# Recurrent attention and a feed-forward block on one core: the first four chunks' feed-forward by weight quarters, a listed order for the prologue, and products of zeros in TensorE's first waits

## The chip, the cores and the metric

The kernel runs on one core of a Trainium2 chip. A core has a matrix engine (TensorE, PE in the profile), VectorE (DVE), ScalarE (ACT), GpSimd (POOL) and a queue engine (SyncE, SP) that issues most of the DMAs here. The metric is the device time in microseconds (us), as the median of several runs. One more run was recorded by the hardware profiler, and all rows quoted here come from such records.

## The reference

The first part is a linear recurrence with a decay, for 4 sequences of 768 steps, 8 heads of 48. The second is a feed-forward block over all 3072 tokens, with `d_model` 384 and `d_ff` 2048.

```python
for t in range(S):
    cur = np.einsum('bhd,bhe->bhde', u[None] * kt, vt)
    y[:, :, t] = np.einsum('bhd,bhde->bhe', rt, state + cur)
    state = wt[:, :, :, None] * state + np.einsum('bhd,bhe->bhde', kt, vt)
x = y.transpose(0, 2, 1, 3).reshape(B * S, H * D)
h = x @ w_in
out = np.maximum(0.01 * h, h) @ w_out
```

Inputs and output are float32 in memory. The kernel's matrix products take bfloat16.

## The kernel before

**Chunks.** Each sequence is cut into chunks of 128 steps, 24 chunks in all. Within a chunk the recurrence becomes matrix products. The steps for one chunk are:

- load w, k, r and v (`load_in`, L470), 192 KB each;
- `lw`, the logarithm of w, on ACT (L332), and its running sum by a product with a triangle matrix, into the one bank `cp`;
- exponentials of the sum, `er` and `ek` (`grow`, L342, ACT), and the products `rk` = r x `er` and k x `ek` (`product`, L348, DVE);
- four transposes each of `rk` on PE (`turn`, L391) and their copies to `rkT` (DVE and ACT); from chunk 12 on a DMA transposes instead;
- scores (L750, or L629 in a pair), masked on DVE (`masked`, L412);
- the state, carried from chunk to chunk: an outer product on PE (L761, L594), `sb` = the decayed state (`shrink`, L421, POOL) and their sum (`state`, L434, DVE);
- the output product (L780 and L785; L646 and L654 in a pair) into the one bank `yp`, and the bonus of u: `ru` twice, `dg` and `vs` (`bonus`, L357 to L369, POOL and DVE), added in `finish` (L444, DVE);
- the transposed result `xT` (L458 on PE, L465 on ACT).

Chunks 0 and 1, and chunks 2 and 3, run as pairs, whose loads take rows of two steps (384 KB a load).

**Feed-forward.** For a chunk there are four *up* quarters and four *down* quarters. An up quarter (L821) is 12 matmuls 128x128, `w_in` against `xT`, into one of the two `hp` banks; ACT applies the leaky ReLU into `g` (L855). A down quarter (L873) is 4 matmuls of 384 columns, `g` against `w_out`, into one of the two `op` banks; after four of them the sum is copied to `o` and stored (L893).

**Weights.** `weight_steps` loads `w_in` and `w_out` in four quarters of 768 KB each, in float32, into buffers of the same ring as the inputs. Each quarter is cast in two halves, one on DVE (L313) and one on ACT (L315). The first down quarter needs the first quarter of `w_out`, the fourth needs the last.

**What sets the order.** Every step is entered in a `Plan` with its engine, an estimated duration, its dependencies and a priority. `Plan.order` runs through the steps in estimated time. On each engine the ready step with the lowest priority number starts next, and the instructions are then emitted in that order. On the chip each engine runs its instructions in the order that they were emitted and waits where an operand isn't there. Attention steps have priorities near ten times the chunk's number, feed-forward steps 1000 and more in an order `seq`: chunk n's ups alternate with chunk n-1's downs. `LEAD` keeps attention at most 8 chunks ahead. `WEIGHTS` tells at which chunk a weight quarter's steps are entered, and with which priority; here one `w_in` quarter comes between the second pair's loads (20.15), the other seven after them (24.0).

```python
PAIRS = (0, 2)
PWIRE, WIRE = 1.45, 1.15
WEIGHTS = [(2, 20.15)] + [(4, 24.0)] * 7
CASTS = 3
```

Of the kernel before, what the change touches and what calls it, by code (L numbers as in the profile page):

```python
# [15 lines left out]
class Plan:  # L16
# [5 lines left out]
    def __init__(self):  # L22
        self.eng, self.dur, self.fn, self.deps, self.pri, self.wire, self.rows = [], [], [], [], [], [], []

    def add(self, eng, dur, fn, deps, pri, wire=None, rows=0):

        i = len(self.eng)
        self.eng.append(eng)
        self.dur.append(dur)
        self.fn.append(fn)  # L30
        self.deps.append(sorted({d for d in deps if d is not None}))
        self.pri.append(pri)
        self.wire.append(wire)
        self.rows.append(rows)
        return i

    def order(self):
# [19 lines left out]
        while events:  # L57
# [13 lines left out]
            free[e] = now + self.dur[i] * (1.8 if e == "PE" and now < 26 else 1)  # L71
            if self.wire[i] is None:
                done[i] = free[e] + self.LAT[e]
            else:

                flying = [x for x in flying if x[0] > free[e]]
                while sum(x[1] for x in flying) + self.rows[i] > 3300:
                    free[e] = max(free[e], flying.pop(0)[0])
                dma_free = max(dma_free, free[e]) + self.wire[i]
                done[i] = dma_free + 1.6  # L80
                flying.append((done[i], self.rows[i]))
# [42 lines left out]
def kernel(  # L124
# [11 lines left out]
    nc = tc.nc  # L136
# [12 lines left out]
    NCI = 3  # L149
# [5 lines left out]
    PWIRE, WIRE = 1.45, 1.15  # L155
    WEIGHTS = [(2, 20.15)] + [(4, 24.0)] * 7
    CASTS = 3
    blocks = [1] * NCH
    assert sum(blocks) == NCH
# [9 lines left out]
    trex = pool.tile([128, 128], BF16, name="trex")  # L169
# [3 lines left out]
    pex = pool.tile([128, 128], BF16, name="pex")  # L173
    halves = pool.tile([128, 2], BF16, name="halves")
# [12 lines left out]
    er_r = ring("er", 3, [128, H, D], F32)  # L187
# [13 lines left out]
    g_r = ring("g", 3, [128, NJ, max(blocks) * L], BF16)  # L201
# [5 lines left out]
    yp_r = pp_r = ring("yp", 1, [128, 512], F32, psum)  # L207
# [3 lines left out]
    with tc.manual_schedule():  # L211
        nc.scalar.preload_act_table_set("natural_log_exp_and_others")

        for t, op in ((trev, ALU.is_ge), (trex, ALU.is_gt)):
# [26 lines left out]
        for q in (0, 64):  # L241
            for i, op in ((slice(0, 64), ALU.is_gt), (slice(64, 128), ALU.is_gt),
# [5 lines left out]
                )  # L248
        nc.vector.memset(onef[:], 1.0)
# [13 lines left out]
        def step(eng, dur, fn, pri, reads=(), writes=(), deps=(), wire=None, rows=0):  # L263
# [4 lines left out]
            i = plan.add(eng, dur, fn, d, pri, wire, rows)  # L268
            for x in (*reads, *writes):
                x.steps.append(i)  # L270
            return i

# [12 lines left out]
        def weight_steps(q, which, pri):  # L285
# [14 lines left out]
            ld = step("SP", 0.45, load, pri, writes=[st], wire=2.0, rows=(384, 512)[which])  # L300
            made = []
            for half, eng in ((0, "DVE"), (1, "ACT")):
                def cast(st=st, q=q, half=half, eng=eng):
# [8 lines left out]
                    if eng == "DVE":  # L312
                        nc.vector.tensor_copy(out=o, in_=i)  # L313
                    else:
                        nc.scalar.copy(out=o, in_=i)  # L315
                d = 0.8 if eng == "DVE" else 0.84
                made.append(step(eng, d, cast, CASTS, reads=[st], deps=[ld]))
# [17 lines left out]
        def cast_v(vb, vn, vl, P0):  # L335
            return step(
                "POOL", 0.57, lambda: nc.gpsimd.tensor_copy(out=vb.t[:], in_=vn.t),  # L337
                P0 + 2, reads=[vn], writes=[vb], deps=[vl])
# [6 lines left out]
        def product(rk, a, xn, e, P0, deps, n):  # L345
            return step(
                "DVE", 0.65 if n < 2 else 0.84 - 0.04 * a,
                lambda: nc.vector.tensor_tensor(out=rk.t[:, a, :, 0:D], in0=xn.t, in1=e.t[:], op=ALU.mult),  # L348
                P0, reads=[xn, e], writes=[rk], deps=deps)

        def bonus(vs, rn, kn, vn, loads, P0):
# [5 lines left out]
                lambda: nc.gpsimd.tensor_tensor(out=ru.t[:], in0=rn.t, in1=ubv, op=ALU.mult),  # L357
                P0 + 2, reads=[rn], writes=[ru], deps=[rl, u_ld])
            s_ruk = step(
                "POOL", 1.05,  # L360
                lambda: nc.gpsimd.tensor_tensor(out=ru.t[:], in0=ru.t[:], in1=kn.t, op=ALU.mult),  # L361
                P0 + 2, reads=[kn, ru], deps=[kl, s_ru])
# [6 lines left out]
                lambda: nc.gpsimd.tensor_tensor(  # L369
                    out=vs.t[:], in0=vn.t, in1=dg.t[:].unsqueeze(2).to_broadcast([128, H, D]), op=ALU.mult),  # L370
                P0 + 2, reads=[vn, dg], writes=[vs], deps=[vl, s_dg])
# [4 lines left out]
        def turn(rk, rkT, s_d, n, P0, banks):  # L376
# [8 lines left out]
            for a, eng in ((0, "DVE"), (1, "ACT")):  # L385
# [10 lines left out]
                def evac(trv=trv, a=a, eng=eng):  # L396
                    o, i = rkT.t[:, a * NP : (a + 1) * NP, :], trv[:, 0:NP, :]
                    if eng == "DVE":
                        nc.vector.tensor_copy(out=o, in_=i)
                    else:  # L400
                        nc.scalar.copy(out=o, in_=i)
# [3 lines left out]
                    eng, 0.42 if eng == "DVE" else 0.585, evac, P0, reads=[tr], writes=[rkT], deps=[s_tr]))  # L405
# [12 lines left out]
        def shrink(sb, s_in, a_ap, use, P0, deps):  # L418
            return step(
                "POOL", 0.92,  # L420
                lambda: nc.gpsimd.tensor_tensor(  # L421
                    out=sb.t[:].rearrange("p g a d -> p (g a) d"),
                    in0=s_in.t[:].rearrange("p g a d -> p (g a) d"),
                    in1=a_ap.rearrange("p g a -> p (g a)").unsqueeze(2).to_broadcast([128, H, D]),
                    op=ALU.mult),
                P0 + 1, reads=[s_in, use], writes=[sb], deps=deps)

        def state(sx, pp, i, sb, P0, deps):

            def f():  # L430
                if sb is None:
                    nc.vector.tensor_copy(out=sx.t[:], in_=i)
# [4 lines left out]
                "DVE", 0.55, f, P0 + 1, reads=[pp] + ([] if sb is None else [sb]), writes=[sx], deps=deps)  # L437

        def finish(yp, vs, s_y, s_vs, n, P0):
# [16 lines left out]
            def typose():  # L456
# [8 lines left out]
                lambda: nc.scalar.copy(out=xT[:, :, col : col + L], in_=trv[:, 0:KT, :]),  # L465
                P0 + 1, reads=[yp], deps=[s_yt]))
# [6 lines left out]
        def spread_u():  # L473
# [4 lines left out]
            up = op_r.take()  # L478
# [12 lines left out]
        def pair(n):  # L491
# [46 lines left out]
            er = [er_r.take() for _ in range(2)]  # L538
            ek = [ek_r.take() for _ in range(2)]
            if n < NCI:  # L540
                cs = [(hp_r if n == 0 else op_r).take() for _ in range(2)]
                s_c = [
                    step("PE", 0.33, lambda: sums(cs[0].t, pev, pev), P0, reads=lw, writes=[cs[0]], deps=s_ln),
                    step("PE", 0.33, lambda: sums(cs[1].t, pex, pex), P0, reads=lw, writes=[cs[1]], deps=s_ln)]
                e_in = [hd(x.t[:, 0:DM]) for x in cs]
                s_w = []
            else:
                cs = [ci_r.take() for _ in range(2)]
                s_c = [
                    step(  # L550
                        "DVE", dve(DM, 120),
                        lambda j=j: nc.vector.tensor_tensor(
                            out=cs[j].t[:], in0=hd(cp.t[:, 0:DM]), in1=lw[j].t[:, :, 0:D],
                            op=(ALU.subtract, ALU.add)[j]),
                        P0, reads=[cp, lw[j]], writes=[cs[j]], deps=[s_cum])
                    for j in range(2)]
                e_in = [x.t[:] for x in cs]
                s_w = s_c
            mid = hd(cp.t[:, 0:DM])
            s_er1 = grow(er[1], cp, mid, 1.0, P0, [s_cum, *s_w])  # L560
            s_ek0 = grow(ek[0], cp, mid, -1.0, P0, [s_cum, *s_w])
            s_er0 = grow(er[0], cs[0], e_in[0], 1.0, P0, [s_c[0]])
            s_ek1 = grow(ek[1], cs[1], e_in[1], -1.0, P0, [s_c[1]])
# [13 lines left out]
            for j in range(2):  # L577
                s_k = product(rk[j], 1, kn[j], ek[j], P0, [kl, (s_ek0, s_ek1)[j]], n)
                s_r = product(rk[j], 0, rn[j], er[j], P0, [rl, (s_er0, s_er1)[j]], n)
# [7 lines left out]
            pps = [op_r.take(), op_r.take()] if n == 0 else [se_r.take(), so_r.take()]  # L587
# [80 lines left out]
        def single(n):  # L668
# [34 lines left out]
            er, ek = er_r.take(), ek_r.take()  # L703
            if n < NCI:
                cq = op_r.take()
                s_ci = step(
                    "PE", 0.17,
                    lambda: nc.tensor.matmul(
                        hd(cq.t[:, 0:DM]), lhsT=trex[:], rhs=lw.t[:, :, 0:D], start=True, stop=True),
                    P0, reads=[lw], writes=[cq], deps=[s_ln])  # L710
                ci, e_in, s_w = cq, hd(cq.t[:, 0:DM]), [s_cum]
            else:
                ci = ci_r.take()
                s_ci = step(
                    "DVE", dve(DM, 120),
                    lambda: nc.vector.tensor_tensor(  # L716
                        out=ci.t[:], in0=hd(cp.t[:, 0:DM]), in1=lw.t[:, :, 0:D], op=ALU.add),
                    P0, reads=[cp, lw], writes=[ci], deps=[s_cum, s_ln])
                e_in, s_w = ci.t[:], [s_cum, s_ci]
            s_er = grow(er, cp, hd(cp.t[:, 0:DM]), 1.0, P0, s_w)  # L720
            s_ek = grow(ek, ci, e_in, -1.0, P0, [s_ci])
            rk = rk_r.take()
            s_r = product(rk, 0, rn, er, P0, [rl, s_er], n)
# [208 lines left out]
```

## Time and profile before

| what | us |
|---|---|
| median of 5 runs | 189.44 |
| lowest and highest of them | 188.65, 192.76 |
| the profiled execution | 188.68 |
| its span, first to last instruction | 187.0 |
| PE busy in the span | 175.0 |
| DVE, ACT, POOL busy | 130.9, 116.2, 109.1 |
| first load issued | 0.80 |
| first up quarter starts | 20.66 |
| first down quarter starts | 27.44 |
| first up quarter of chunk 4 starts | 50.13 |

A page of the profile gives the busy time of each engine, the span in 40 slices with the busy tenths of each engine, the chain of waits that ended last, and the costliest groups of instructions. A group's row names the line, the engine, the operation, what is written and read, how many there are, their busy time and the mean of one. The engine timelines give start and length of single instructions; a bracket at the end of a line is the idle time before it and what ended it. `SPq` is SyncE issuing a DMA. A matmul's end is modelled, so where matmuls follow each other their starts tell more than their lengths.

### The profile page before, as it was taken

To read this page: it belongs to the slowest core of one execution; us is meant where nothing else is said; L and a number is where in the kernel's file an instruction comes from. 1 tells how busy PE (TensorE), PEld (TensorE's weight loads), DVE (VectorE), ACT (ScalarE), POOL (GpSimd) and SP (SyncE) were. 2 spreads that over 40 slices of the span, in tenths; PEclk is the share of its full clock that TensorE was granted. 3 is DMA by queue.
4 is the path that set the end of the run, shared out by engine and by line. 5 is a ranking of instruction groups with operands and counts; after the bars stand their busy time and mean duration, and the time that the engine had idled before them with its cause. 6 is when DMAs were issued, how large, how long until landed. Compare 5 with 4: busy or idle time off the path is not lost.

```text
span 187.0 us, 6219 instructions
## 1 busy us (share of the span) xinstructions
PE 175.0 (94%) x2550; PEld 137.3 (73%) x2550; DVE 130.9 (70%) x226; ACT 116.2 (62%) x254; POOL 109.1 (58%) x148
## 2 busy tenths in 40 slices
PE   3678879999999999999999999999999999999992
PEld 1256767788778878788787787878887877877871
DVE  2399796777779888877967999766987868441111
ACT  2746686678876877796687666676374645334430
POOL 7799923277969798978792885172637644500000
PEclk9999999999999999999999999999999999999999
DMA  6999999999988897987899779998789995512102
GB/s 154 261 316 325 369 381 300 195 190 222 189 194 176 178 227 155 217 195 174 173 210 188 147 164 230 143 177 190 139 189 174 172 206 124 123 44 67 38 7 84
DMA packets 116383, 34.62 MB, mean 185 GB/s; under 512 B 109697, under 2 KB 114818, under 8 KB 116354
## 3 DMA queue, kind: packets, MB, share of 16 engines
q1 hardware_dynamic: 116352, 34.22, 84.2%
q8 instruction: 20, 0.33, 0.7%
q14 instruction: 9, 0.07, 0.1%
q10 hardware_dynamic: 2, 0.00, 0.0%
HBM read 25.17 MB, written 4.72 MB: 160 GB/s over the span
## 4 chain that ended last, share of the span: by engine, by line
PE 84%; SPq 7%; DMA 6%; DVE 1%; issue 0%
PE op L873 34%; PE hp L821 33%; DMA in<-in_moe_w_out_dram 6%; SPq L470 4%; PE se L750 3%; SPq L290 3%; PE yp L785 2%; PE cp L691 2%; PE yp L761 2%; PE yp L780 2%; PE se L391 1%; PE so L391 1%; PE yp L458 1%; PE cp L696 1%; DVE w_out_b L313 1%; PE yp L654 1%
## 5 line engine op out<-in xcount | busy, mean ns | idle before, releaser
L855 ACT ACTIVATE g<-hp 128x512 bf16<-128x512 f32 x96 | 57.0, 596 | 43.5 <-PE hp L821 42.5
L821 PE MATMUL hp<-xT,w_in_b 128*128 128x128 bf16 x1152 | 79.7, 220 | 0.1
L873 PE MATMUL op<-w_out_b,g 128*128 128x384 bf16 x384 | 76.5, 326 | 1.0 <-DVE w_out_b L313 1.0
L821 PEld LDWEIGHTS <-w_in_b 128*128 128x128 bf16 x1152 | 69.9, 98 | 7.1 <-DVE w_in_b L313 0.2
L873 PEld LDWEIGHTS <-g 128*128 128x128 bf16 x384 | 33.0, 97 | 15.8 <-issue 1.1
L357 POOL TENSOR_TENSOR ru<-in,ub 128x384 f32<-128x384 f32 x24 | 26.7, 1111 | 14.2 <-DMA in<-in_r_dram 14.1
L369 POOL TENSOR_TENSOR vs<-in,dg 128x384 f32<-128x384 f32 x24 | 20.2, 843 | 17.6 <-DVE dg L365 13.9
L361 POOL TENSOR_TENSOR ru<-ru,in 128x384 f32<-128x384 f32 x24 | 25.8, 1077 | 0.9
L421 POOL TENSOR_TENSOR sb<-s,a 128x384 bf16<-128x384 f32 x17 | 15.7, 926 | 16.4 <-DVE s L434 12.9
L348 DVE TENSOR_TENSOR rk<-in,er 128x384 bf16<-128x384 f32 x24 | 19.3, 803 | 7.5 <-DMA in<-in_r_dram 5.6
L348 DVE TENSOR_TENSOR rk<-in,ek 128x384 bf16<-128x384 f32 x24 | 23.3, 970 | 1.4 <-ACT a L738 0.9
L412 DVE TENSOR_TENSOR m<-se,maskb 128x512 bf16<-128x512 f32 x20 | 13.7, 687 | 7.5 <-PE so L750 6.9
L444 DVE TENSOR_TENSOR y<-yp,vs 128x384 bf16<-128x384 f32 x24 | 13.3, 552 | 7.7 <-PE yp L785 4.8
L889 DVE COPY o<-op 128x384 f32<-128x384 f32 x10 | 5.6, 556 | 17.1 <-PE op L873 17.0
L337 POOL CAST vb<-in 128x384 bf16<-128x384 f32 x24 | 15.4, 646 | 0.9 <-DMA in<-in_v_dram 0.9
L332 ACT ACTIVATE lw<-in 128x384 bf16<-128x384 f32 x24 | 12.4, 520 | 2.8 <-DMA in<-in_w_dram 2.6
L365 DVE TENSOR_REDUCE dg<-ru 128x8 f32<-128x384 f32 x24 | 12.9, 542 | 1.1 <-POOL ru L361 1.1
L412 DVE TENSOR_TENSOR m<-so,maskb 128x512 bf16<-128x512 f32 x20 | 13.6, 679 | 0.0
L342 ACT ACTIVATE er<-cp 128x384 f32<-128x384 f32 x22 | 10.8, 492 | 3.5 <-DVE ci L716 3.0
L716 DVE TENSOR_TENSOR ci<-cp,lw 128x384 f32<-128x384 f32 x20 | 11.0, 549 | 1.5 <-ACT g L855 0.9
L342 ACT ACTIVATE ek<-ci 128x384 f32<-128x384 f32 x20 | 10.5, 524 | 0.0
L391 PEld LDWEIGHTS <-rk 128*128 128x128 bf16 x96 | 6.9, 105 | 4.8 <-DVE rk L348 4.0
(103 smaller groups left out, 193.2 us busy)
## 6 DMA issues: line engine op xcount, KB each, us to landing
out_dram<-o SPq DMA_DIRECT2D x24, 192.0 KB, 2.2
in<-in_w_dram SPq DMA_DIRECT2D x20, 192.0 KB, 3.6
in<-in_k_dram SPq DMA_DIRECT2D x20, 192.0 KB, 3.8
in<-in_r_dram SPq DMA_DIRECT2D x20, 192.0 KB, 3.7
in<-in_v_dram SPq DMA_DIRECT2D x20, 192.0 KB, 3.5
in<-in_moe_w_in_dram SPq DMA_DIRECT2D x4, 768.0 KB, 8.5
in<-in_moe_w_out_dram SPq DMA_DIRECT2D x4, 768.0 KB, 12.4
in<-in_w_dram SPq DMA_DIRECT2D x2, 384.0 KB, 5.1
```

The lines of the kernel that those rows point to most:

```text
L337: "POOL", 0.57, lambda: nc.gpsimd.tensor_copy(out=vb.t[:], in_=vn.t),
L342: "ACT", 0.5, lambda: nc.scalar.activation(out=out.t[:], in_=i, func=AF.Exp, scale=scale),
L348: lambda: nc.vector.tensor_tensor(out=rk.t[:, a, :, 0:D], in0=xn.t, in1=e.t[:], op=ALU.mult),
L357: lambda: nc.gpsimd.tensor_tensor(out=ru.t[:], in0=rn.t, in1=ubv, op=ALU.mult),
L361: lambda: nc.gpsimd.tensor_tensor(out=ru.t[:], in0=ru.t[:], in1=kn.t, op=ALU.mult),
L369: lambda: nc.gpsimd.tensor_tensor(out=vs.t[:], in0=vn.t, in1=dg.t[:].unsqueeze(2).to_broadcast([128, H, D]), op=ALU.mult),
L412: lambda par=par: nc.vector.tensor_tensor(out=m.t[:, par], in0=gt(sc[par].t), in1=mask.unsqueeze(1).to_broadcast([128, NP, 128]), op=ALU.m ...
L421: lambda: nc.gpsimd.tensor_tensor(out=sb.t[:].rearrange("p g a d -> p (g a) d"), in0=s_in.t[:].rearrange("p g a d -> p (g a) d"), in1=a_ap ...
L444: lambda: nc.vector.tensor_tensor(out=y.t[:], in0=hd(yp.t[:, 0:DM]), in1=vs.t[:], op=ALU.add),
L821: nc.tensor.matmul(hp.t[:, a * N : (a + 1) * N], lhsT=w_in_b[:, t, (j + a) * 128 : (j + a + 1) * 128], rhs=xT[:, t, c0 : c0 + N], start=(a ...
L855: lambda hp=hp, g=g, j=j, J=J, N=N: nc.scalar.activation(out=g.t[:, j : j + J, 0:N], in_=hp.t[:, 0 : J * N].rearrange("p (a n) -> p a n", ...
L873: nc.tensor.matmul(op.t[:, 0:DM], lhsT=g.t[:, j, off : off + 128], rhs=w_out_b[:, j, :], start=(j == 0), stop=(j == NJ - 1))
```

## The change

**Feed-forward order.** For chunks 0 to 3 the order `seq` is written out in `FIRST`, as (0 for up or 1 for down, chunks, quarters). Chunks 0 and 1 take each weight quarter in turn, then chunk 2 and chunk 3 follow. From chunk 4 on the alternation is as before, but chunk 3's downs no longer alternate with chunk 4's ups. The `g` ring grows from three buffers to four.

**Prologue.** `EARLY` is a list of step numbers. Its steps get priorities below all others in the order listed, and a letter behind a number moves the step to ACT (a), DVE (v) or POOL (p). `step` takes the engines that are possible with their estimated durations (`alts`), and helpers `copy` and `times` emit an operation on the engine chosen. All eight weight quarters are entered at chunk 4. The order of loads on SP becomes: w, k, r, v of the first pair; v, w, k, r of the second; `w_in` quarters 1 and 0, `w_out` 0, `w_in` 2 and 3, `w_out` 1, 2 and 3; then w, r of chunk 4, w of chunk 5, k and v of chunk 4.

**Exponentials in place.** The `er` ring is gone. ACT writes the exponential into the PSUM bank from which it read the sum (`cp`, or the bank of the pair's second sum), and DVE's product with r reads it there. `ek` of one chunk of a pair is likewise written in place. The bank is held until the product has read it. The second pair gets one sum by a product (in `op`'s first bank) and one by a DVE addition; before, both were products. The constant `trex` is gone. The first pair's two outer products go to `op`'s first bank and `yp`; before, to both `op` banks.

**Zeros.** While steps are emitted, each gap that the plan has on PE before `WARM` (24 us) is filled to 70% with products of a zero tile, 256 columns each, into `op`'s second bank. The program has 60 of them, all but two ahead of the first up quarter.

**Estimates.** Some of the plan's durations and rates are different (`PWIRE`, `wire`, the PE factor 1.8 until 6 rather than 26).

```diff
-            free[e] = now + self.dur[i] * (1.8 if e == "PE" and now < 26 else 1)
+            free[e] = now + self.dur[i] * (1.8 if e == "PE" and now < 6 else 1)
...
-    WEIGHTS = [(2, 20.15)] + [(4, 24.0)] * 7
-    CASTS = 3
+    WEIGHTS = [(4, 24.0)] * 8
+    WARM = 24.0
+    CASTS = 21
+
+    EARLY = """
+        0 4 1 2 3 5 8 61 7 6 12 58 11 16 13 14 15 21 32 59 17 23 24 18 20p 19 22 28 9a 60 29 30 10a 33
...
+    """
+    FIRST = [(0,(0,1),(0,1,2,3)),(1,(0,1),(0,1)),(0,(2,),(0,)),(1,(0,1),(2,)),(0,(2,),(1,)),(1,(0,1),(3,)),(0,(2,),(2,3)),(0,(3,),(0,)),(1,(2,),(0,)),(0,(3,),(1,)),(1,(2,),(1,)),(0,(3,),(2,)),(1,(2,),(2,)),(0,(3,),(3,)),(1,(2,),(3,)),(1,(3,),(0,1,2,3))]
...
-    g_r = ring("g", 3, [128, NJ, max(blocks) * L], BF16)
+    g_r = ring("g", 4, [128, NJ, max(blocks) * L], BF16)
...
+        def copy(e, o, i):
+            if e == "ACT":
+                nc.scalar.copy(out=o, in_=i)
+            else:
+                (nc.vector if e == "DVE" else nc.gpsimd).tensor_copy(out=o, in_=i)
+
+        def times(e, o, a, b):
+            (nc.vector if e == "DVE" else nc.gpsimd).tensor_tensor(out=o, in0=a, in1=b, op=ALU.mult)
...
-            er, ek = er_r.take(), ek_r.take()
-            if n < NCI:
...
+            ci, ek = ci_r.take(), ek_r.take()
...
+            er = View(cp, hd(cp.t[:, 0:DM]))
+            s_er = grow(er, cp, er.t, 1.0, P0, [s_cum, s_ci])
+            s_ek = grow(ek, ci, ci.t[:], -1.0, P0, [s_ci])
...
         seq = []
-        for nb in range(len(blocks) + 1):
+        for kind, cs, qs in FIRST:
+            for q in qs:
+                for c in cs:
+                    seq.append((kind, c, made[c][kind][q]))
+        for nb in range(4, len(blocks) + 1):
             a = made[nb][0] if nb < len(blocks) else []
             bq = made[nb - 1][1] if nb else []
+            if nb == 4:
+                bq = []
...
+        for rank, word in enumerate(EARLY.split()):
+            i = int(word.rstrip("avp"))
+            plan.pri[i] = rank - 10000
+            if word[-1] in "avp":
+                plan.eng[i] = {"a": "ACT", "v": "DVE", "p": "POOL"}[word[-1]]
+                plan.dur[i] = plan.alts[i][plan.eng[i]]
+
+        at = 0.8
         for i in plan.order():
-            plan.fn[i]()
+            if plan.eng[i] == "PE" and at < WARM:
+                for _ in range(int((plan.start[i] - at) * 0.7 / 0.13)):
+                    nc.tensor.matmul(
+                        op_r.tiles[1][:, 0:256], lhsT=zeros[:, 0:128], rhs=zeros[:], start=True, stop=True)
+                at = plan.start[i] + plan.dur[i]
+            if plan.alts[i]:
+                plan.fn[i](plan.eng[i])
+            else:
+                plan.fn[i]()
```

## Prediction, made before the changed kernel ran

> **What bounds the kernel now.** I read the page's slices first, then the chain of waits, then single engines in order of time.
>
> ```profile
> PE   3678879999999999999999999999999999999992
> PEclk9999999999999999999999999999999999999999
> DMA  6999999999988897987899779998789995512102
> GB/s 154 261 316 325 369 381 300 195 190 222 189 194 176 178 227 155 217 195 174 173 210 188 147 164 230 143 177 190 139 189 174 172 206 124 123 44 67 38 7 84
> ```
>
> A slice is 4.7 us. From the seventh on (about 28 us) TensorE (PE) is full up to the last slice; only the first six have holes. So in the steady part nothing but PE work counts, and a change to the prologue pays only by the PE work that it gets done sooner. DMA is full from the second slice until the weights are in.
>
> ```profile
> 15.17 11.03 DMA in<-in_moe_w_out_dram
> 26.23 1.17 DVE w_out_b L313
> 27.44 0.81 PE op L873 x4
> 28.25 0.67 PE hp L821 x12
> ...
> 180.32 3.26 PE op L873 x20
> 183.61 0.56 DVE o L889
> ```
>
> The chain in order of time (start, length, what). It runs over loads until the first quarter of `w_out` lands and is cast, and is PE from 27.44 on. PE ends at 183.6; a copy and a store make 3.4 us more, to 187.0. An up-projection quarter (12 matmuls) costs 0.67, a down quarter (4) 0.65.
>
> ```profile
> 20.00 0.83 ACT L315 CAST w_in_b<-in 128x768 bf16<-128x768 f32 x1 [1.18 <-DMA in<-in_moe_w_in_dram]
> 22.02 0.83 ACT L315 CAST w_in_b<-in 128x768 bf16<-128x768 f32 x1 [0.53 <-DMA in<-in_moe_w_in_dram]
> 26.22 0.83 ACT L315 CAST w_out_b<-in 128x768 bf16<-128x768 f32 x1 [0.37 <-DMA in<-in_moe_w_out_dram]
> 32.62 0.83 ACT L315 CAST w_out_b<-in 128x768 bf16<-128x768 f32 x1 [0.35 <-DMA in<-in_moe_w_out_dram]
> ```
>
> ScalarE's casts in order of time; the bracket says that each waited for its load. Quarters of 768 KB land 2.1 us apart, the last of eight at 32.6.
>
> ```profile
> 20.66 1.49 PE L821 MATMUL hp<-xT,w_in_b 128*128 128x128 bf16 x12
> 23.27 0.83 PE L821 MATMUL hp<-xT,w_in_b 128*128 128x128 bf16 x12
> ```
>
> PE in order of time: the same 12 matmuls take 1.49 us at 20.66 and 0.83 at 23.27, though the clock row shows 9 throughout. So PE ran at half rate until about 22 us and the granted-clock row doesn't tell it; I go by the durations.
>
> Now what PE has to do after 27.44 in the kernel before: 183.6 - 27.4 = 156.1 us, with no releaser shown in it. Done by then: four up quarters, no down quarter, all of the first pair's attention, of the second pair the sums and transposes.
>
> **The change part by part.**
>
> *Order of loads.* The new SP order is both pairs' inputs, then `w_in` quarters 1 and 0, `w_out` 0, `w_in` 2 and 3, `w_out` 1, 2, 3. Before, the second pair's r and v went behind `w_in` 0, and all of `w_out` behind all of `w_in`. The same bytes lie ahead of the last quarter, so it lands at 32.6 again. Counting back by 2.1: `w_out` 2 and 1 at 30.5 and 28.4, `w_in` 3 and 2 at 26.3 and 24.2, `w_out` 0 at 22.1 (before: 26.2), `w_in` 0 and 1 at 20.0 and 17.9. No bytes are saved; only the order is. SP also carries chunk 4's loads straight behind, as before.
>
> *Feed-forward by quarters.* Before, chunk 0's up quarters waited one by one for `w_in`, and its first down for 26.2. Now two chunks use each quarter as it lands. Both halves of `w_in` 0 must be cast: 20.0 + 0.83 = 20.9 for the first up. Its other conditions are chunk 0 and 1's `xT` and what stands ahead on PE (both pairs' transposes, the second pair's outer product). Chunk 0's `xT` was written at 18.3 before, chunk 1's at 23.2. What chunk 1 waits for is VectorE (DVE): its second half of masks, second products and y. Its order now holds, from the first mask to the y of chunk 1 and its half of the `w_in` 0 cast: four masks, one state sum, one `ci`, two y, one reduction, two products, one `ru`, one evacuation, one shrink, one cast. At the start-to-start pitches of the rows before (0.61 a mask, 0.46 to 0.48 a y, sum or PSUM product, 0.33 an evacuation, about 0.8 for the two with both inputs in SBUF, 0.6 a cast) this is 8.6 us. Before, masks began at 13.7; two of the four products of the first pair took 1.35 us each beside a busy POOL, and now read one input from PSUM, and one is on POOL: 1.5 to 2 us sooner, so 12.0 + 8.6 = 20.6. Loads and DVE meet within 0.3 us. I take **20.9** for the first up.
>
> *The ledger.* At the first up PE still has before's 156.1, plus the four up quarters (4 x 0.67 = 2.7), less the second pair's outer product, which has moved ahead (28.85 to 29.30, 0.45), plus two zero products (0.11 each at 56 ns per 128 columns): 158.6.
>
> *Idle behind the first up.* Four ups end at 23.6. The first down needs `w_out` 0, whose halves are both cast on POOL; a POOL cast of 384 columns takes 0.505, so 768 about 1.0, two 2.0: 24.1. PE waits 0.5. Then scores, a down, ups of quarter 2 (25.2, there), the second pair's masked products, ups of quarter 3 (27.3, there): full. Chunk 2's `xT` copy stands on DVE behind the cast of `w_out` 1, which lands at 28.4: 28.4 + 0.6 + 0.4, about 29.8 with the transposes; its ups come up on PE at about 30.6. Full again, but in-order PE has some ten such meetings; I give them 0.5 more. Idle **1.0**.
>
> *Zeros.* 60 products of 256 columns, all but two ahead of the first up. [...] By the row, PE busy 4.3 of 5 us in 15 to 20 still ran slow at 20.66. [...] Against them: 22 stand ahead of the first sums; slow, one is 0.21 us, so 4.7 us plus the bonus row's own 1.6 end at about 7, against 5.3 for the sums before. If warm by 5 us, at 6.3, and the sums themselves (2.3 us before) halve: level. I take 0, with 0 to 1.5 for the range.
>
> *Exponentials written to PSUM* (in place, no `er` ring). No row shows ScalarE writing PSUM; reading PSUM to SBUF it takes 0.49. I take 0.49, ends 0.4 and 0.6; six of them in the prologue, 0.6 us at most, partly on the path. Later it is hidden by full PE, as is the longer hold of the one `cp` bank: the next chunk's sums wait for the product instead of the exponential, some 0.6 us more in a cycle of 6.6 us per chunk. If that cover went, PE would stand behind each `cum`: 0.6 x 20 = 12 us, but it would need DVE a whole chunk late.
>
> ```profile
> L348 DVE TENSOR_TENSOR rk<-in,er x24: 547/746/1346, 7.8 to 159.2; 128x384 bf16<-128x384 f32 x24
> L348 DVE TENSOR_TENSOR rk<-in,ek x24: 536/1004/1378, 8.3 to 155.8; 128x384 bf16<-128x384 f32 x24
> L357 POOL TENSOR_TENSOR ru<-in,ub x24: 992/1001/1370, 7.8 to 155.6; 128x384 f32<-128x384 f32 x24
> ```
>
> *Spreading over engines* (least, median and greatest ns per tile). [...] By the row DVE's own k product has a median of 1.00 beside a busy POOL, and POOL's 1.00: nothing lost, a DVE slot won. I take the row. ScalarE's share (v casts, the first state) stands in 1.0 to 1.9 us waits that it had between 8 and 18.
>
> *Fewer constants and sums:* `trex` (0.5 us of POOL) and four matmuls go; hidden by the wait for the first w. The fourth g buffer only keeps ups from waiting.
>
> *What is late next: chunk 4.* Feed-forward of chunks 0 to 3 (16 ups, 16 downs: 21.1), the second pair's rest (about 3), chunk 4's attention and part of 5's (about 3) end near 20.9 + 27 + 1 = 49. Chunk 4's loads follow the weights: k and v at about 37; then DVE's ten steps for chunks 4 and 5, transposes, scores, y: 44.5 to 46. Before, its `xT` came at 48.7 with no hurry. Two us of margin.
>
> **Sum:** 20.9 + 158.6 + 1.0 = 180.5, and 3.4 for the tail: span 183.9 against 187.0, **3.1 us less**. The profiled execution took 188.68; the median shown is 189.44. 189.4 - 3.1 = **186.3**.
>
> **Rivals.**
> 1. *Chunk 4 comes late* (0.16). The margin of 2 us goes; for it: `w` and k land only after 33, and DVE holds both chunks' `ru`. Against it: PE has 12 us of other work. At 51 instead of 49: 188.4, within no change (within 0.5%, 188.5 to 190.4, is what this kernel's measurement can't tell from nothing) or just below it.
> 2. *Zeros don't warm PE or stand in its way* (0.08): 186.3 + 1.0 = 187.3.
> 3. *POOL becomes the bound, slower* (0.11). Ahead of the first up its queue holds ten two-input steps, then a `w_in` 1 half and both `w_out` 0 halves, in order. At the row's greatest, 1.37 instead of 1.0, this is 3.7 us: rk of the second pair, vs and y of chunk 1 late, first up at 24.6, first down at 27.5. Then 24.6 + 158.6 + 1.4 + 3.4 = 188.0, that is 190.4; it decides from a first up at 24.0. For: the second pair's k, vs and y all pass through POOL. Against: fewer DVE steps with two SBUF inputs now run beside it.
> 4. *No idle at all, and the steady part loses nothing to early waits* (0.13): first up at 20.0, idle 0: 184.4; with chunk 2 early and the first pair's ups sooner 183.5.
>
> **How the numbers follow.** Forecast 0.52 (185.0 to 187.8). Faster: 0.52 + 0.08 + 0.13 + a fifth of rival 1 = 0.76. Same: most of rival 1, 0.13. Slower: 0.11. The range reaches from rival 4 to rival 3: 183.4 to 190.2.
>
> **What would show it.** First up with `w_in` near 20.9 at 0.8, not 1.5; first down near 24; chunks 0 and 1 sharing each quarter; last `w_out` cast still at 32.6; chunk 4's first up at 47 to 49 without a gap (before: 50.1); PE full from there, with 133 us to its end. Wrong if the first up is after 22, if PE idles between 24 and 49 by over 2 us, or if steady stretches show PE waiting for `cp`.

## The result, and the profile after

| | before | after |
|---|---|---|
| median (us) | 189.16 | 188.13 |
| lowest, highest | 188.57, 192.76 | 187.09, 188.88 |
| the profiled execution | 188.68 | 188.07 |
| its span | 187.0 | 186.4 |
| PE's last product ends | 183.57 | 182.97 |
| first up quarter starts | 20.66 | 22.25 |
| first down quarter starts | 27.44 | 25.11 |
| chunk 4's first up starts | 50.13 | 50.05 |

The medians are of all runs of each kernel, 39 and 20. The ratio is 0.9936, with a 95% interval of 0.9917 to 0.9955: 0.6% or 1.0 us (189.16 - 188.13) faster, where 3.1 was forecast. The direction held and the size did not; 188.13 lies inside the range.

The changed kernel's page, the span in 40 slices of 4.7 us, busy tenths:

```profile
PE   7999997999999999999999999999999999999892
PEclk9999999999999999999999999999999999999999
DMA  6999999789598997897999886989999999351202
```

PE, which had 3 6 7 8 8 7 in its first six slices, now has 7 9 9 9 9 9. Much of that is the zeros, which count as busy. Two slices further on are not full, though: the seventh (28 to 33 us), and the one before the last two (175 us). The chain of waits of the changed kernel (start, length, what) shows what is in them:

```profile
1.12 2.74 PE op L933 x12
3.86 1.57 PE op L504 x2
5.44 2.25 PE op L933 x10
...
29.30 1.45 PE hp L837 x24
31.09 1.12 issue
32.62 0.76 PE op L898 x4
...
169.97 1.26 issue
171.82 3.71 DMA xT<-y
175.57 1.51 PE hp L837 x24
179.72 3.26 PE op L898 x20
```

The chain now begins with the zeros (L933) and no longer with weight loads. At 31.09 PE stands for 1.12 us with nothing named that it waits for, in the middle of one block of score products (L652). At 175.57 it has waited for the last chunk's `xT`.

PE in order of time, the changed kernel's first 8 us:

```profile
1.12 2.74 PE L933 MATMUL op<-zeros 128*128 128x256 bf16 x12 [1.12 <-DVE zeros L268]
3.79 1.64 PE L504 MATMUL op<-ur,onef 1*128 1x384 f32 x2
5.37 2.31 PE L933 MATMUL op<-zeros 128*128 128x256 bf16 x10
7.47 0.85 PE L544 MATMUL hp<-lw,pev 128*128 128x384 bf16 x2
```

L504 is the row for the bonus, L544 the first pair's sums. Ten zeros of 256 columns take 2.10 us from the first one's start to the next step's: 0.21 each, half rate (where PE is full, 128 columns take 57 ns, so 256 take 0.11). The first sums, which started at 5.29 before, wait behind them until 7.47. What follows from the sums is late too: the first product with r at 8.87 (7.80 before), chunk 1's `xT` at 22.25, and with it the first up:

```profile
22.25 1.50 PE L837 MATMUL hp<-xT,w_in_b 128*128 128x128 bf16 x24
25.11 0.81 PE L898 MATMUL op<-w_out_b,g 128*128 128x384 bf16 x4
...
50.05 1.51 PE L837 MATMUL hp<-xT,w_in_b 128*128 128x128 bf16 x24
```

Here 24 matmuls take 1.50, where before 12 took 1.49: this is full rate. The groups of the changed kernel, for the steps whose cost was a guess (busy us and mean ns of one behind the first bar):

```profile
L370 ACT ACTIVATE cp<-cp 128x384 f32<-128x384 f32 x22 | 10.6, 482 | 6.3 <-DVE ci L729 6.3
L300 DVE TENSOR_TENSOR rk<-in,cp 128x384 bf16<-128x384 f32 x22 | 12.1, 548 | 3.0 <-ACT cp L370 2.4
L300 POOL TENSOR_TENSOR rk<-in,ek 128x384 bf16<-128x384 f32 x4 | 4.0, 1001 | 10.8 <-ACT ek L370 10.8
```

To see when work is gained and lost, I summed what PE had done by each time, every product at the mean time from its start to the next one's where PE is full (57 ns for 128 columns, 165 for 384), the zeros and the bonus row at nothing. The table is an estimate in us of work; its last row is the end of PE's work.

```
by      before   after   lead
40       22.1     23.1    1.0
50       32.1     33.1    1.0
174     156.2    157.2    1.0
end     183.57   182.97   0.6
```

The lead is 1.0 us where the prologue is over, and constant from there to 174: the steady part neither wins nor loses. The changed kernel also has 0.3 less to do in all, since two products of the sums are gone (the prediction had four); so of 1.3 us some 0.7 go at the end.

### The profile page after: what moved, and what is told of

Read it like the earlier page. It is cut to its first block, busy times and chain, and to the rows that moved or that the text cites. A ratio compares the mean times of both kernels' runs of the same rounds, so it can differ in the third digit from the quotient of the medians.

```text
span 186.4 us, 6316 instructions
## 1 busy us (share of the span) xinstructions
PE 179.3 (96%) x2608; PEld 140.4 (75%) x2608; DVE 120.1 (64%) x232; ACT 115.9 (62%) x254; POOL 101.1 (54%) x142
## 4 chain that ended last, share of the span: by engine, by line
PE 89%; DVE 3%; DMA 2%; issue 2%; ACT 1%; POOL 1%
PE hp L837 34%; PE op L898 32%; PE op L933 3%; PE se L764 3%; PE yp L799 2%; DMA xT<-y 2%; PE cp L714 2%; PE yp L775 2%; PE yp L794 1%; PE so L418 1%; DVE m L436 1%; PE se L418 1%; POOL rk L300 1%; PE yp L481 1%; PE yp L677 1%
## 5 line engine op out<-in xcount | busy, mean ns | idle before, releaser
L837 PE MATMUL hp<-xT,w_in_b 128*128 128x128 bf16 x1152 | 77.9, 219 | 0.5 <-DMA xT<-y 0.5
L837 PEld LDWEIGHTS <-w_in_b 128*128 128x128 bf16 x1152 | 68.5, 98 | 7.0 <-DMA xT<-y 0.9
L300 POOL TENSOR_TENSOR ru<-in,ub 128x384 f32<-128x384 f32 x22 | 23.1, 1052 | 6.6 <-DMA in<-in_r_dram 6.5
L300 POOL TENSOR_TENSOR vs<-in,dg 128x384 f32<-128x384 f32 x22 | 18.9, 859 | 8.6 <-DVE dg L393 8.4
L300 POOL TENSOR_TENSOR ru<-ru,in 128x384 f32<-128x384 f32 x20 | 20.8, 1041 | 0.9
L300 DVE TENSOR_TENSOR rk<-in,ek 128x384 bf16<-128x384 f32 x18 | 13.0, 724 | 3.7 <-ACT ek L370 2.5
L370 ACT ACTIVATE cp<-cp 128x384 f32<-128x384 f32 x22 | 10.6, 482 | 6.3 <-DVE ci L729 6.3
L300 DVE TENSOR_TENSOR rk<-in,cp 128x384 bf16<-128x384 f32 x22 | 12.1, 548 | 3.0 <-ACT cp L370 2.4
L933 PE MATMUL op<-zeros 128*128 128x256 bf16 x60 | 11.6, 328 | 1.1 <-DVE zeros L268 1.1
L297 POOL CAST vb<-in 128x384 bf16<-128x384 f32 x19 | 10.2, 539 | 0.5 <-DMA in<-in_v_dram 0.5
```

The costliest lines, as they stand in the source:

```text
L297: (nc.vector if e == "DVE" else nc.gpsimd).tensor_copy(out=o, in_=i)
L300: (nc.vector if e == "DVE" else nc.gpsimd).tensor_tensor(out=o, in0=a, in1=b, op=ALU.mult)
L370: "ACT", 0.5, lambda: nc.scalar.activation(out=out.t[:], in_=i, func=AF.Exp, scale=scale),
L837: nc.tensor.matmul(hp.t[:, a * N : (a + 1) * N], lhsT=w_in_b[:, t, (j + a) * 128 : (j + a + 1) * 128], rhs=xT[:, t, c0 : c0 + N], start=(a ...
L933: nc.tensor.matmul(op_r.tiles[1][:, 0:256], lhsT=zeros[:, 0:128], rhs=zeros[:], start=True, stop=True)
```

## The experiments

**1. No zeros.**

```diff
-    WARM = 24.0
+    WARM = 0.0
```

> No zero products at all (60 fewer matmuls, 120 fewer PE instructions with their weight loads); nothing else changed. Three theories. Fetch (PE between 13 and 32 us is paced by the arrival of its instructions, 256 at a time, some 6.5 us apart, because the fetch stands behind the weight loads in the same 16 DMA engines): the holes of 0.56 us at 18.7 and 1.25 us at 31.0 are gone. Delay (the first 22 zeros, run at half rate, hold the first sums from 5.3 to 7.5): the first sums start at 5.3 again and the first up comes before 22.25, near 21. Warmth (the zeros are what makes the first ups fast): sums and first ups run at half rate, an up pair takes 2.6 instead of 1.35. Fetch and delay together would give up to 2.5 us, warmth takes 1 to 1.5 back: 186.6 to 188 against 188.1 for the changed kernel. If only warmth counts, it is slower than the changed kernel, 189 or more.

186.38 (186.05 to 187.07), ratio 0.9842 (0.9797 to 0.9887): 1.75 us faster than the changed kernel. PE in order of time:

```profile
5.44 0.80 PE L544 MATMUL hp<-lw,pev 128*128 128x384 bf16 x2 [1.62 <-ACT lw L360]
...
21.51 0.20 PE L617 MATMUL se<-vb,rk 64*128 64x96 bf16 x1 [0.45 <-ACT rkT L295]
...
21.96 3.03 PE L837 MATMUL hp<-xT,w_in_b 128*128 128x128 bf16 x48
```

The sums wait for `lw` alone and start 2.0 us sooner. The first up gains only 0.3, because PE runs at half rate until 20.26: the second pair's transposes take 0.61, not 0.40, their copies to `rkT` on ACT end later, and PE waits 0.45 for these before the outer product that stands ahead of the first up. By then the rate is full: 48 matmuls take 3.03. The lead over before at 40 us is 2.6 (24.7 against 22.1), not 1.0: the zeros cost more than half of what the rest of the change wins.

Of the 2.1 us by which PE's work ends sooner here (180.86), 0.3 come from the first up and 1.1 from the stand at 31 us, which is 0.18 here; 0.8 come from the end, where PE doesn't wait.

**2 to 4. Only the first 22 zeros left out; zeros half as many and twice as wide; twice as many and half as wide.** The second was to separate the delay of the sums from the rest. The other two keep the columns and change the number of instructions.

```diff
-for _ in range(int((plan.start[i] - at) * 0.7 / 0.13)):
+for _ in range(int((plan.start[i] - at) * 0.7 / 0.13) if plan.start[i] > 5.8 else 0):
```

```diff
-zeros = pool.tile([128, 256], BF16, name="zeros")
+zeros = pool.tile([128, 512], BF16, name="zeros")
...
-for _ in range(int((plan.start[i] - at) * 0.7 / 0.13)):
+k = int((plan.start[i] - at) * 0.7 / 0.13)
+for c in (512,) * (k // 2) + (256,) * (k % 2):
...
-    op_r.tiles[1][:, 0:256], lhsT=zeros[:, 0:128], rhs=zeros[:], start=True, stop=True)
+    op_r.tiles[1][:, 0:c], lhsT=zeros[:, 0:128], rhs=zeros[:, 0:c], start=True, stop=True)
```

```diff
-for _ in range(int((plan.start[i] - at) * 0.7 / 0.13)):
+for _ in range(2 * int((plan.start[i] - at) * 0.7 / 0.13)):
...
+    op_r.tiles[1][:, 0:128], lhsT=zeros[:, 0:128], rhs=zeros[:, 0:128], start=True, stop=True)
```

> The 22 zero products ahead of the first sums are left out, the other 38 stay. Delay: first sums at 5.3, and the first up some 1 us earlier than 22.25, time 187 to 187.5. Warmth: the sums run at half rate (2.3 us instead of about 1.4), so little is won at the first product of DVE (8.87), and the first up stays within 0.3 of 22.25; PE is at full rate by the first up all the same. Fetch: 44 fewer PE instructions, so the hole at 31.0 is later or smaller.

> The same zero columns in 36 products, most of them 512 wide, instead of 60 of 256: the same PE time, 48 fewer PE instructions. Fetch: the boundaries between blocks of 256 instructions are reached later, at about 19.5 to 20, 26.3 and 33, so the holes shrink from 0.56 and 1.25 to less than half; time 0.5 to 1.2 us less than the changed kernel. Delay and warmth: no change, since neither PE time nor place of the zeros differs.

> The same zero columns in 120 products of 128 columns instead of 60 of 256: the same PE time, 120 more PE instructions. Fetch: three blocks of 256 have to come before the same work is done, each some 6.5 us after the other while DMA is full, so PE stands for 2 to 3 us more between 13 and 32 us; time 1 to 3 us more than the changed kernel. Delay and warmth: no change.

Without the first 22: 186.95 (186.76 to 187.30), ratio 0.987 (0.983 to 0.991). The sums start at 5.42, the first up at 21.14. That is 1.1 us off the first up and 1.2 off the time, with the stand at 31 us still there: the delay nearly by itself.

Wide: 187.43 (186.84 to 188.05), not clear of the changed kernel. The stand, expected to shrink to less than half, is 1.14 there. Narrow: 186.98 (186.45 to 187.52), although 60 products more, 120 instructions with their weight loads, had been expected to cost time. PE with narrow zeros:

```profile
1.12 2.74 PE L933 MATMUL op<-zeros 128*128 128x128 bf16 x24 [1.12 <-DVE zeros L268]
3.79 0.91 PE L504 MATMUL op<-ur,onef 1*128 1x384 f32 x2
4.63 1.29 PE L933 MATMUL op<-zeros 128*128 128x128 bf16 x20
5.76 0.49 PE L544 MATMUL hp<-lw,pev 128*128 128x384 bf16 x2
...
32.82 0.27 PE L677 MATMUL yp<-vb,m 64*64 64x48 bf16 x6
34.33 0.59 PE L677 MATMUL yp<-vb,m 64*64 64x48 bf16 x26 [1.24 <-issue]
```

Two readings. The first zeros take 2.74 as in the changed kernel, but the later ones 1.29 for the same columns that took 2.31. The trace's record of granted clock has the full rate from 3.78 here, and from 8.32 in the changed kernel, for the same columns from the same start. And the stand at 31 us is gone; there is one at 32.9 instead, between other instructions. So the stand is tied neither to a time nor to what PE computes. I counted PE's instructions (matmuls and weight loads) up to each stand: it comes after 961 of them in the changed kernel and with wide zeros, after 1217 with narrow ones, which are 256 apart.

The page of the changed kernel has a DMA queue for these (packets, MB, share):

```profile
q8 instruction: 20, 0.33, 0.7%
```

0.33 MB in 20 packets are 16 KB each. Set beside PE's instructions, the packets give this table (us):

```
kernel              after     PE had passed   packet          PE stands
                    number    256 earlier     from, to        from, to
changed              961        25.88         29.60  30.67    30.90  32.21
no zeros             961        28.11         30.75  31.85    33.14  33.32
first 22 left out    961        25.35         29.04  30.17    30.35  31.58
narrow zeros        1217        27.91         31.33  32.78    32.91  34.33
```

Each packet starts 2.6 to 3.7 us after PE has passed the number before, takes 1.1 to 1.5, and PE goes on 1.4 to 1.6 later. So from one number to the next PE needs 5.2 to 6.4 us here, where its own work between them takes 5.0 in each row. In the no-zeros kernel the packet waited least, and PE stands 0.18. In the kernel before, PE takes over 9 us from one number to the next up to 32 us (13.63, 23.16, 32.23), and there is no stand at them.

**5. Sixty zeros of two columns and one row: the instructions without the work.**

```diff
-op_r.tiles[1][:, 0:256], lhsT=zeros[:, 0:128], rhs=zeros[:], start=True, stop=True)
+op_r.tiles[1][0:1, 0:2], lhsT=zeros[:, 0:1], rhs=zeros[:, 0:2], start=True, stop=True)
```

> The 60 products stay where they are, but each is one row and two columns: the PE instructions of the changed kernel, 120 more than without zeros, and next to no PE time. Fetch: the hole at the block boundary comes back (PE instruction number 961, reached at about 30.4, stands for about 1.2 us), so about 1.2 us more than without zeros (186.4): 187.3 to 187.9. Delay: no early delay, so the time of the kernel without zeros, 186.4. Warmth: PE is as cold as without zeros, 186.4.

188.70 (186.75 to 189.56), ratio 0.9967 (0.9934 to 1.000). The stand expected at number 961 did not come. PE:

```profile
22.82 2.43 PE L837 MATMUL hp<-xT,w_in_b 128*128 128x128 bf16 x24
25.28 0.90 PE L837 MATMUL hp<-xT,w_in_b 128*128 128x128 bf16 x13
```

The first pair of ups takes 2.43, not 1.50: half rate, until 24.78 by the record. PE comes to number 961 only at 32.4, later than its packet. This run tests the fetch poorly, but it shows what a slow PE costs at the ups: 0.9 us in the first pair alone. It gives no theory its forecast: 188.70 lies above all three. Why the full rate came 4.5 us later than with no zeros at all stays open.

**6. Zeros only where the plan is past 12 us, 512 wide (17 products).** If what hurts is the early zeros and what helps is a warm PE at the first up, this takes one without the other.

```diff
-zeros = pool.tile([128, 256], BF16, name="zeros")
+zeros = pool.tile([128, 512], BF16, name="zeros")
...
-for _ in range(int((plan.start[i] - at) * 0.7 / 0.13)):
-    nc.tensor.matmul(
-        op_r.tiles[1][:, 0:256], lhsT=zeros[:, 0:128], rhs=zeros[:], start=True, stop=True)
+k = int((plan.start[i] - at) * 0.7 / 0.13) if plan.start[i] > 12 else 0
+for c in (512,) * (k // 2) + (256,) * (k % 2):
+    nc.tensor.matmul(
+        op_r.tiles[1][:, 0:c], lhsT=zeros[:, 0:128], rhs=zeros[:, 0:c], start=True, stop=True)
```

> Zeros only from 12 us on (none ahead of the first pair's sums, transposes and scores) and 512 columns wide: some 17 products. Delay, warmth and fetch together: first sums at 5.4, PE at full rate by 18 or so, first up at about 21.2 instead of 22.0 without zeros, no hole of over 0.5 us at 30 to 32, since instruction 961 is reached only after 32: 185.4 to 186.1, less than without zeros (186.4). If warmth at the first up is worth nothing, 186.4 or more.

**186.08** (185.89 to 186.35), ratio 0.9829 (0.9802 to 0.9856), the lowest median and faster than both kernels, but not clear of no zeros at all (0.9842). What a warm PE is worth at the first up is not shown by it. PE:

```profile
21.48 1.51 PE L837 MATMUL hp<-xT,w_in_b 128*128 128x128 bf16 x24 [0.59 <-DVE w_in_b L297]
...
32.60 0.56 PE L837 MATMUL hp<-xT,w_in_b 128*128 128x128 bf16 x7 [0.51 <-issue]
```

The first up waits for a weight again and not for attention. The stand is 0.72 from start to start, where at most 0.5 had been expected.

**7. No zeros, and feed-forward in the order of before.** `FIRST` goes, and so do the steps of `EARLY` from number 713 on, the feed-forward ones.

```diff
-for kind, cs, qs in FIRST:
-    for q in qs:
-        for c in cs:
-            seq.append((kind, c, made[c][kind][q]))
-for nb in range(4, len(blocks) + 1):
+for nb in range(len(blocks) + 1):
...
+            if i >= 713:
+                continue
```

> No zeros, and the feed-forward of the first four chunks in the order of the kernel before (chunk n's ups alternating with chunk n-1's downs), its steps no longer listed in EARLY; the listed order of loads, attention and casts stays. If the order by quarters is what brings PE work forward, chunk 1's ups wait behind chunk 0's third and fourth quarter (cast at about 25.3 and 27.2), some two up quarters (1.3 us) fewer are done at 28, and some of it is lost for good: 187.5 to 189, against 186.4 without zeros. If the earlier attention of the second pair is what counts, within 0.5 us of 186.4.

187.98 (187.48 to 190.00), ratio 0.9938 (0.9912 to 0.9964). PE:

```profile
20.55 1.26 PE L837 MATMUL hp<-xT,w_in_b 128*128 128x128 bf16 x12
22.36 0.84 PE L837 MATMUL hp<-xT,w_in_b 128*128 128x128 bf16 x12
...
26.13 0.84 PE L837 MATMUL hp<-xT,w_in_b 128*128 128x128 bf16 x12 [0.49 <-DVE w_in_b L297]
```

One chunk uses up a quarter in 0.84, and the next comes 1.8 to 3.8 us after. So the parts can be told apart. By ratios against before: prologue without zeros and without the new order 0.9938 (1.2 us won), the order by quarters 0.9842 beside it (1.8 us won), the zeros 0.9936 instead of 0.9842 (1.8 us lost). Together they make the changed kernel's ratio, as they must, since each is a difference between two runs. The first part is everything else in the change and isn't told apart further.

**8 to 10. The changed kernel again, three times.** In the runs so far the time of the full rate, and the hole at the end, had changed from kernel to kernel without a reason in the edit.

> The changed kernel, unchanged, for one more look. Theory (the zeros' cost depends on when the full clock is granted; the stand at the 961st TensorE instruction belongs to the program): first sums between 6.0 and 7.5 us, later the later the full rate comes; TensorE stands 1.1 to 1.4 us at its 961st instruction near 31 us in every look. Rival (both are one execution's accident): first sums at 5.4 to 5.8 us or no stand near 31 us. The hole at chunk 23's xT near 174.8 us: a matter of the transpose's latency, so present in some looks only.

> The changed kernel, unchanged, second look: as for the first. Theory: the time follows first sums and tail hole, about 187 us where the full rate comes before 5 us, 188 where it comes after 8; the stand at the 961st instruction is there again, 1.1 to 1.4 us. Rival: it is gone here or the times don't follow.

> The changed kernel, unchanged, third look: as for the first two.

The four recorded executions of the same program (the repeats are one execution each, on a chip where the kernel before took 190.04):

```
                              the first   again 1   again 2   again 3
time                           188.07     186.28    187.52    188.15
full rate from                   8.32       4.46      3.82      9.12
first sums                       7.47       6.04      5.73      7.47
first up                        22.25      20.96     21.13     22.28
packet for number 961 ends      30.67      29.32     30.04     30.52
PE goes on at                   32.21      30.76     31.52     31.94
its stand (start to start)       1.31       0.66      0.69      1.01
last xT issued                 171.82     170.38    171.13    171.54
landed after                     3.7        3.3       3.8       4.0
PE stands for it                 0.76       0.37      0.88      1.10
PE's work ends                 182.97     181.15    182.41    183.03
```

PE of the first repeat:

```profile
1.12 2.74 PE L933 MATMUL op<-zeros 128*128 128x256 bf16 x12 [1.12 <-DVE zeros L268]
3.79 1.22 PE L504 MATMUL op<-ur,onef 1*128 1x384 f32 x2
4.94 1.26 PE L933 MATMUL op<-zeros 128*128 128x256 bf16 x10
6.04 0.49 PE L544 MATMUL hp<-lw,pev 128*128 128x384 bf16 x2
...
20.96 1.51 PE L837 MATMUL hp<-xT,w_in_b 128*128 128x128 bf16 x24 [0.22 <-DVE w_in_b L297]
...
24.32 0.81 PE L898 MATMUL op<-w_out_b,g 128*128 128x384 bf16 x4 [0.32 <-POOL w_out_b L297]
```

Ten zeros take 1.26, not 2.31; the two sums 0.49, not 0.85. The first up then waits for a cast, 0.22, and starts at 20.96. So this cost of the zeros belongs to an execution and not to the program: the first up comes 1.1 to 1.3 us later where the full rate comes at 8 to 9 us than where it comes near 4.

The time doesn't follow from that alone. The second repeat had the rate earliest and took 187.52: its first down waited 0.89 for POOL's cast of `w_out` 0 (0.32 in the first repeat), and PE stood 0.88 at the end. Its first sums, at 5.73, also lie below the 6.0 expected, where I had put the rival; but the stand at number 961, which the rival denied, is there.

The stand at number 961 is there in all four, as expected, but at 0.66 and 0.69 in two of them it is below the 1.1 that I had put as its least: PE goes on 1.42 to 1.54 us after the packet's end in every one, and how long it stands depends on how early it came. Of the twenty times of the changed kernel, two are no longer than the 187.52 of the second repeat and sixteen are above 187.9, so the late grant would be by far the commoner case, if the times go by it as in these four.

## Why the prediction was wrong in size

**The step that failed is *Zeros*: "I take 0".** It had the case written down ("slow, one is 0.21 us, so 4.7 us plus the bonus row's own 1.6 end at about 7"), and that is what happened: 7.47. I had set against it that PE would be "warm by 5 us", and that the sums themselves would then halve. That zeros bring the full rate by 5 us was not shown: of four executions of the program it came at 3.82 and 4.46 in two, and only at 8.3 and 9.1, after the sums had waited, in the others. That wait is the first up at 22.25 instead of 20.9, 1.35 us. That the products in front cause the delay is shown by leaving these 22 out (experiment 2: first up 21.14), and that it hangs on the grant by the same program with an early one: 20.96 and 21.13. The term's 0 is not what the runs showed: by medians all zeros together cost 1.75 us (experiment 1). And the slow first ups that they were to save were hardly there without them: the full rate came at 20.26 in experiment 1 and at 21.43 in experiment 7. Rival 2 was this mechanism; its 1.0 us, which no run shows, was too small, and so was its chance.

That the kernel without zeros meets the forecast (186.4 and 186.3) is in part luck: its first up came 1.1 us later than 20.9, and PE's idle time behind it, put at 1.0, was under 0.2.

**Idle behind the first up, "1.0": 1.36.** That is what is left of the sum below, and the stand at number 961 alone is 1.31 of it. The prediction had the wait for `w_out` 0 and ten small meetings here, and nothing for PE's own instructions. The wait for `w_out` that I had counted (0.5) did not arise in the profiled execution, since the ups came later.

**The end of PE's work, put at no wait: 0.76.** I took PE to be full up to its end. The "3.4" behind that held (182.97 to 186.4). The last chunk's `xT` was issued at 168.45 before, 7.1 us ahead of its use; in the changed kernel at 171.82, 3.0 ahead of when PE was done with the rest. The transpose by DMA then landed after 3.7. In all four executions PE had 3.0 us, and stood for what the landing took beyond that; with no zeros it landed after 2.3, and PE did not stand. With the old order of feed-forward (experiment 7) it was issued at 167.32, and PE did not stand either: the margin went with the order by quarters. Why the landing takes 2.3 in one run and 4.0 in another is open. So the sum for the profiled execution: 22.25 + 158.6 + 1.36 + 0.76 = 182.97, which is where PE ends.

**Right:**
- The *ledger*: without zeros, with PE idle for under 0.2, the first up to PE's end took 158.9, where 158.6 was forecast. In all later stages the lead is constant, so nothing steady was lost to the longer hold of `cp`.
- *Exponentials to PSUM*: 482 ns measured, 0.49 taken. The product that reads it takes 548 ns, where its like took 803 in the mean before (547 to 1346). None of the 22 took over 555: with one operand in PSUM it didn't slow down here beside a POOL that was busy for 101.1 us of the span.
- *Spreading over engines*: POOL's pair products took 1.00, as by the row. Beside DVE's 0.55 that is nearly twice as long, and about what DVE's k product took before (1.00 in the median). Rival 3, POOL as the bound, didn't come: the first up never waited for POOL, the first down by up to 0.9 in one execution.
- *Feed-forward by quarters*: 1.8 us by experiment 7, the largest single gain. PE was warm at the first up, as forecast (1.50 a pair, where experiment 5's slow one took 2.43), but it was so in experiment 1 too.

**Chunk 4** came at 50.05 and not at 47 to 49, but not as rival 1 had it: PE was full ahead of it, with 14 down quarters done instead of 12. It is the lost lead, and no wait of its own.

## What to carry to other kernels

Filler products meant to keep PE at full rate belong where nothing that others wait for stands behind them: in a queue in order, at half rate, they cost twice what they cost warm (0.21 us each against 0.11), and in four executions of one program the rate came at four different times. Here the kernel without any was as fast, within noise, as the best with some. A stretch of many small matmuls in the shade of large loads should be checked against the arrival of the instructions themselves: PE stood for up to 1.4 us here. When one engine is made full up to the end, its last feeder's margin has shrunk too: look there before adding up the gain.

## What the runs showed of the hardware

**PE stood behind packets of the instruction queue.** The changed kernel's page has 20 packets of 16 KB on the queue q8, named instruction, and PE ran 5216 instructions, 261 for each packet. While the weights load, the packets of the table above waited 2.6 to 3.7 us, took 1.1 to 1.5, and PE went on 1.4 to 1.6 after their end; stands of up to 1.4 us followed, at numbers 256 apart, whatever instructions stood there. Why the packet waits so long stays open. The loads are the likely reason: behind the last weight cast (34.3) in the changed kernel, PE passed number 1217 at 37.91 and the next packet started at 38.36, 0.5 us later. But no run took the loads away, and full DMA alone isn't enough: in the kernel before, PE passed number 449 at 23.16 and the next packet started 0.6 us later, with DMA as full (a share of 1.04 from 20 to 25 us, and 1.07 from 25 to 30 in the changed kernel).

**The full rate came 2.7 to 8.0 us after the first product,** in four executions of one program (3.82, 4.46, 8.32, 9.12, from a start at 1.12).

The record of the granted clock says more. Its stretch at full rate lasts 180.91 us in the two early executions, 177.49 in the two late ones and 163.84 in the kernel before. These differ by 3.42 and 13.65 us, one and four times 3.41, so in these five executions the rate changed as if at steps of 3.41 us, and their place against the program's start differed from one execution to the next. Nor did busy time decide, if the steps are counted back from the full rate, an estimate from these lengths. In the changed kernel's first execution PE was busy for the whole step from 1.49 to 4.90, and the full rate didn't follow; in the second repeat it was busy for 79% of the step from 0.41 to 3.82, and it did. The former held 1.1 us of the bonus row's products, which the trace gives as 1*128 where the zeros have 128*128. That this is the difference is suggested by these executions and not tested.

The clock row of the page shows 9 all the same: for the first microseconds the durations have to be read.
